# Squares and norms of an input check moved into the last product of a fused attention and feed-forward kernel

## The chip, the cores and the metric

The kernel runs on one core of a Trainium2 chip. A core has a matrix engine (TensorE, PE in the profile; its weight loads are PEld), a vector engine (VectorE, DVE), an activation engine (ScalarE, ACT), a general engine (GpSimd, POOL) and a sequencer for transfers (SyncE, SP). Each engine works through its own list of instructions in order and waits where an instruction needs something that another engine has not finished. Matrix products are summed in PSUM, a small memory in banks of 128 x 512 numbers of 32 bits; everything else on the chip is in SBUF. The metric is the device time of one execution in microseconds (us), and the median of several executions is compared.

## The reference

There are 8 batches of 576 tokens with 8 heads of 64. Attention sees a window of 32 positions to each side; 8 global positions see everything and are seen by everything. The result, 4608 tokens of 512 numbers, goes through a feed-forward layer with a periodic activation:

```python
scores = scale * np.matmul(q, k.transpose(0, 1, 3, 2))
mask = np.abs(pos[:, None] - pos[None, :]) <= window
mask = mask | is_global[:, None] | is_global[None, :]
scores = np.where(mask, scores, -1000000000.0)
attn = softmax(scores)                       # written out, with 1e-09 on the sum
x = np.matmul(attn, v)                       # then heads side by side: 4608 x 512

h = x @ w_in                                 # 512 x 2048
s = np.sin(alpha * h)
g = h + s * s / (alpha + 1e-09)
out = g @ w_out                              # 2048 x 512
```

## The kernel before, in words

The kernel walks over the batches in an order that is written out by hand. For batch b it does the attention (`attention(b, ...)`), then the first product with the activation (`gemm1(b)`), and the second product (`gemm2(b)`) is not done at once: it is a generator of single matmuls that stands in the list `waiting`. `fill(n)` takes n matmuls from that list and issues them, so that TensorE has something to do while the attention of the next batch waits for ACT and DVE. Attention b+1 thus runs with the second product of batch b in its gaps; `phase_a(b_att, b_moe)` sets up such a pair, and its inner function `beside(at)` issues small side jobs after head pair `at`.

**The first product** runs over 16 groups `nt` of 128 columns of w_in. A group takes 8 matmuls into one of three pairs of banks (`zn`, `zd`, and a third called `zr`), then a Sin on ACT out of PSUM, a square on ACT or DVE, and a multiply-add on DVE that writes H2, the input of the second product.

**The second product** takes blocks of 128 tokens: 16 matmuls of 512 columns into one of two banks, `zo[0]` or `zo[1]` in turn, then a copy `osb` on ACT (line 1048) and one or two output writes from SP (line 1055). The first matmul of a block waits until the copy two blocks earlier has emptied its bank. The generator issues a block's copy only when the matmul after it is asked for. After the last batch nothing is left to fill around: the rest of the second product of batch 6 (18 matmuls) and the five blocks of batch 7 (80 matmuls) run alone, followed by `gemm2_globals`, 16 matmuls for the global tokens, a copy, and an indirect write from POOL.

**The check.** Sin, exponentials and reciprocals are computed in a way that holds for moderate inputs only. So the kernel gathers evidence, and if any of it fails, it computes everything again in a slow general way (`general_path`). The pieces of that evidence are what the change moves:

- `square_w(c)`, four times: ACT squares a quarter of w_in, 2048 numbers per partition (line 888), and from the second on DVE adds the square to W2 (line 890). Before the change the first two stand in the first product of batch 1 (lines 995 and 996), the other two in attention 2 (lines 1132 and 1133).
- `column_norms`: 16 matmuls of one column sum W2 over partitions (line 895); five small DVE instructions make of it `limit`, the largest squared length that a token may have. It stands in attention 3 (lines 1119 and 1120).
- `square_x(b, part)`: DVE squares the tokens of a batch and halves them three times into SR, 288 columns (320 in the last batch, which carries the global tokens). This stays where it is.
- `token_norms(b, ...)`: one matmul sums SR over partitions, and DVE compares it with `limit` and counts (line 933). For batches 0 to 3 it stands in attentions 4 to 7 (lines 1121 and 1122), for batches 4 to 7 in the last product, after 32 of its matmuls.
- `judge`: a chain of small DVE instructions joins all evidence into one number, a matmul (line 952) sums it, and DVE writes `verdict`. It stands 16 matmuls further on. At the end every engine loads the verdict (line 1174) and branches (line 1175).

The end of the program before, for reference:

```python
    waiting.append(gemm2(B - 1))
    square_x(B - 1, 0)
    square_x(B - 1, 1)
    fill(32)
    for n, b in enumerate(sorted(SR)):
        token_norms(b, (zn, zd)[n % 2][:, 0, :])
    fill(16)
    judge(zn[:, 0, :])
    fill(2 * NT * NT)
    gemm2_globals()
```

Of the kernel before, what the change touches and what calls it, by code (L numbers as in the profile page):

```python
# [10 lines left out]
ALU = mybir.AluOpType  # L11
AF = mybir.ActivationFunctionType
DT = mybir.dt
# [3 lines left out]
P = 128  # L17
# [230 lines left out]
def kernel(  # L248
# [11 lines left out]
    nc = tc.nc  # L260
    B, H, S, D = q.shape
    DM, DFF = moe_w_in.shape
# [4 lines left out]
    CT = DM // P  # L267
    NT = DFF // P
    HALF = S // 2
# [11 lines left out]
    mctx = ExitStack()  # L281
    mctx.enter_context(tc.manual_schedule())
    dramp = mctx.enter_context(tc.tile_pool(name="dramp", bufs=2, space=bass.MemoryType.DRAM))
    main = mctx.enter_context(tc.tile_pool(name="main", bufs=1))
# [3 lines left out]
    xpool = mctx.enter_context(tc.tile_pool(name="xpool", bufs=1))  # L288
    spool = mctx.enter_context(tc.tile_pool(name="spool", bufs=3))
    osbp = mctx.enter_context(tc.tile_pool(name="osbp", bufs=3))  # L290
    srp = mctx.enter_context(tc.tile_pool(name="srp", bufs=4))

    VX = [main.tile([P, NHP, NT12, P], DT.bfloat16, name=f"VX{i}") for i in range(2)]
    KX = [main.tile([P, NHP, NT12, P], DT.bfloat16, name=f"KX{i}") for i in range(2)]
# [19 lines left out]
    limit = main.tile([P, 1], DT.float32, name="limit")  # L314
    EA = main.tile([P, B * NHP * 3], DT.float32, name="EA")
    RA = main.tile([P, B * NHP], DT.float32, name="RA")
    XC = main.tile([P, B], DT.float32, name="XC")
    XCG = main.tile([P, 1], DT.float32, name="XCG")


# [563 lines left out]

    def square_w(c):

        t = SQ[:, 0:DFF] if c else W2[:]
        nc.scalar.activation(out=t, in_=w_in[:, c, :], func=AF.Square)
        if c:
            nc.vector.tensor_tensor(out=W2[:], in0=W2[:], in1=t, op=ALU.add)  # L890
# [14 lines left out]
        )  # L905
        nc.vector.reciprocal(out=limit[:], in_=limit[:])

    SR = {}

    def square_x(b, part):  # L910

        W = HALF + (NE if b == B - 1 else 0)
        n = 2 * CT * W
        if part == 0:
            xf = xTs[b][:].rearrange("p c e s -> p (c e) s")[:, :, 0:W]
            nc.vector.tensor_tensor(
                out=SQ[:, 0:n].rearrange("p (g s) -> p g s", s=W), in0=xf, in1=xf, op=ALU.mult
            )
            return
        for m in (n // 2, n // 4):  # L920
            nc.vector.tensor_tensor(out=SQ[:, 0:m], in0=SQ[:, 0:m], in1=SQ[:, m : 2 * m], op=ALU.add)
        n //= 8
        SR[b] = srp.tile([P, n], DT.bfloat16, name="SR" if b < B - 1 else "SRl")
        nc.vector.tensor_tensor(out=SR[b][:], in0=SQ[:, 0:n], in1=SQ[:, n : 2 * n], op=ALU.add)

    def token_norms(b, pn):

        n = SR[b].shape[1]
        nc.tensor.matmul(out=pn[:, 0:n], lhsT=ones[:], rhs=SR.pop(b)[:], start=True, stop=True)
        for lo, hi, dst in ((0, HALF, XC[:, b : b + 1]), (HALF, n, XCG[:, 0:1])):  # L930
            if hi > lo:
                low = normp.tile([P, hi - lo], DT.bfloat16, name="low" if hi == HALF else "lowg")
                nc.vector.tensor_scalar(
                    out=low[:], in0=pn[:, lo:hi], scalar1=limit[:, 0:1], scalar2=0.0, op0=ALU.is_le,
                    op1=ALU.add, accum_out=dst,
                )

    def judge(pv):

        ok = [normp.tile([P, 1], DT.float32, name=f"ok{i}") for i in range(4)]  # L940
        for i, (src, lim, op) in enumerate(
            ((EA, LIM_SUM, ALU.is_le), (RA, LIM_REC, ALU.is_le), (XC, HALF - 0.5, ALU.is_ge),
             (XCG, NE - 0.5, ALU.is_ge))
        ):
            t = normp.tile(list(src.shape), DT.float32, name=f"cmp{i}")
            nc.vector.tensor_scalar(out=t[:], in0=src[:], scalar1=lim, scalar2=None, op0=op)
            nc.vector.tensor_reduce(out=ok[i][:], in_=t[:], axis=AX.X, op=ALU.min)
        nc.vector.tensor_tensor(out=ok[0][:], in0=ok[0][:], in1=ok[1][:], op=ALU.mult)
        nc.vector.tensor_tensor(out=ok[2][:], in0=ok[2][:], in1=ok[3][:], op=ALU.mult)
        okb = normp.tile([P, 1], DT.bfloat16, name="okb")  # L950
        nc.vector.tensor_tensor(out=okb[:], in0=ok[0][:], in1=ok[2][:], op=ALU.mult)
        nc.tensor.matmul(out=pv[:, 0:1], lhsT=ones[:], rhs=okb[:], start=True, stop=True)
        nc.vector.tensor_copy(out=verdict[:], in_=pv[:, 0:1])
# [6 lines left out]
    def gemm1(b):  # L960


        xT = xTs[b]
        r0 = (b % 2) * S
        more = b == B - 1
        W = HALF + (NE if more else 0)
        hr = tc.alloc_tile_pool(name="hr", bufs=1, space=PSUM)
        hs = {}

        order = "nrdonrdonrdnrdon" if b == 0 else "nrd" * 5 + "n"  # L970

        def chunks(nt, cs):
            if nt not in hs:
                if order[nt] == "o":
                    hs[nt] = [(slice(e, e + 1), zo[e][:, None, :]) for e in range(2)]
                else:
                    h = {"n": zn, "d": zd}.get(order[nt]) or hr.tile([P, 2, 512], DT.float32, name="zr")
                    hs[nt] = [(slice(0, 2), h[:])]
            h = [ap[:, i] for es, ap in hs[nt] for i in range(es.stop - es.start)]
            for c in cs:  # L980
                for e in range(2):
                    lhsT = w_in[:, c, nt * P : (nt + 1) * P]
                    nc.tensor.matmul(  # L983
                        out=h[e][:, 0:W], lhsT=lhsT, rhs=xT[:, c, e, 0:W],
                        start=(c == 0), stop=(c == CT - 1), skip_group_check=True,
                    )

        on_act = (ON_ACT_FIRST, ON_ACT_SECOND, ON_ACT)[min(b, 2)]
        for nt in range(NT):
            if b < 2 and 10 <= nt < 14:  # L990
                for which, t, y in PLACES[2 * (nt - 10) : 2 * (nt - 9)]:
                    place(b + 1, which, t, y, nc.vector.tensor_copy, slice(0, NHP if b else 2))
            if b == 1 and nt in (3, 4):
                square_x(0, nt - 3)
            if b == 1 and nt in (6, 8):
                square_w(nt // 2 - 3)
            if b == 0 and nt == 11:
                turn_kq()
            if b == 0 and nt == 11:

                load_w_out()
                cast_globals_v()
                place_globals(1)
                load_v(1, (2, 3))
                load_vg(1)
            if nt == 0:

                for n in range(2):
                    chunks(n, range(CT - 1))
            chunks(nt, range(CT - 1, CT) if nt < 2 else range(CT))  # L1010
            fill((GROUP_LATE if b == 1 else PER_GROUP)[nt])
            sb = spool.tile([P, 2, HALF + NE], DT.bfloat16, name="sb")
            s2 = spool.tile([P, 2, HALF + NE], DT.bfloat16, name="s2")
            for es, h in hs[nt]:
                nc.scalar.activation(  # L1015
                    out=sb[:, es, 0:W], in_=h[:, :, 0:W], func=AF.Sin, scale=alphaT[:, nt : nt + 1]
                )
            if nt in on_act:
                nc.scalar.activation(out=s2[:, :, 0:W], in_=sb[:, :, 0:W], func=AF.Square)  # L1019
            else:  # L1020
                nc.vector.tensor_tensor(out=s2[:, :, 0:W], in0=sb[:, :, 0:W], in1=sb[:, :, 0:W], op=ALU.mult)  # L1021
            for es, h in hs[nt]:
                nc.vector.scalar_tensor_tensor(  # L1023
                    out=H2[:, nt, r0 : r0 + S].rearrange("p (e c) -> p e c", e=2)[:, es],
                    in0=s2[:, es, 0:HALF], scalar=recipT[:, nt : nt + 1], in1=h[:, :, 0:HALF],
                    op0=ALU.mult, op1=ALU.add,
                )
            if more:
                nc.vector.scalar_tensor_tensor(
                    out=HG[:, nt, :].rearrange("p (x n) -> p x n", x=2),  # L1030
                    in0=s2[:, :, HALF:W], scalar=recipT[:, nt : nt + 1], in1=hs[nt][0][1][:, :, HALF:W],
                    op0=ALU.mult, op1=ALU.add,
                )
        hr.release()
# [43 lines left out]
    def fill(n):  # L1078
        while n and waiting:
            if next(waiting[0], None) is None:  # L1080
                waiting.pop(0)
            else:
                n -= 1
# [16 lines left out]
    def phase_a(b_att, b_moe):  # L1100
        def beside(at):

            if b_moe is None:
# [11 lines left out]
                    load_v(1, (0, 1))  # L1115
                    gather(v, gv)
                return
            if at == 0:
                if b_moe == 2:
                    column_norms(zn[:, 0, :])  # L1120
                if b_moe >= 3:
                    token_norms(b_moe - 3, zn[:, 1, :])
            if 0 <= at < 2 and b_moe:
                square_x(b_moe, at)
            if b_att == 1 and at == 0:
# [3 lines left out]
                place(b_att + 1, which, t, y, nc.vector.tensor_copy)  # L1129
            if b_moe == 0 and at == 2:  # L1130
                turn_qk(2)
            if b_moe == 1 and at in (2, 3):
                square_w(at)

        if b_moe is not None:
            waiting.append(gemm2(b_moe))
# [25 lines left out]
    waiting.append(gemm2(B - 1))  # L1162
    square_x(B - 1, 0)
    square_x(B - 1, 1)
    fill(32)
    for n, b in enumerate(sorted(SR)):
        token_norms(b, (zn, zd)[n % 2][:, 0, :])
    fill(16)
    judge(zn[:, 0, :])
    fill(2 * NT * NT)  # L1170
    gemm2_globals()
    mctx.close()

# [33 lines left out]
```

## Time and profile before

| What | Value |
|---|---|
| Median of 3 runs | 372.3 us (371.79 to 372.88) |
| Profiled execution, its own time | 373.89 us |
| Span of the profiled execution | 372.2 us |
| TensorE busy | 336.6 us, 90% of the span |
| ACT busy | 293.5 us, 79% |
| DVE busy | 282.8 us, 76% |
| Mean granted TensorE clock | 0.994 of full speed |
| Second product, line 1042 | 143.3 us, 530 matmuls recorded |
| Squares of w_in, line 888 | 4 instructions of 1.89 to 1.91 us, the first from 82.4 us, the last from 117.1 us |
| First sums of norms in the last product | from 346.29 us |

A span runs from the first to the last recorded instruction; the execution's own time contains it and some time around it. The busy time of an engine is an average over stages that are limited by different things, so it says little about a single move. The profile's timeline lists instructions in order of time: start, duration, engine, line, what is written from what, and in brackets how long the engine stood idle before and which engine released it. A matmul's duration includes its way through the array, so that matmuls overlap; their pace is read from start to start. Batches start their attention, by the first score matmul, at 98.69 (batch 2), 141.64, 181.19, 220.26, 259.44 and 298.61 us (batch 7).

### The profile page before, as it was taken

To read this page: it belongs to the slowest core of one execution; us is meant where nothing else is said; L and a number is where in the kernel's file an instruction comes from. 1 tells how busy PE (TensorE), PEld (TensorE's weight loads), DVE (VectorE), ACT (ScalarE), POOL (GpSimd) and SP (SyncE) were. 2 spreads that over 40 slices of the span, in tenths; PEclk is the share of its full clock that TensorE was granted. 3 is DMA by queue.
4 is the path that set the end of the run, shared out by engine and by line. 5 is a ranking of instruction groups with operands and counts; after the bars stand their busy time and mean duration, and the time that the engine had idled before them with its cause. 6 is when DMAs were issued, how large, how long until landed. Compare 5 with 4: busy or idle time off the path is not lost. (4 is left out here: it accounts for less than half of the span.)

```text
span 372.2 us, 8377 instructions
## 1 busy us (share of the span) xinstructions
PE 336.6 (90%) x2994; PEld 228.8 (61%) x3040; DVE 282.8 (76%) x624; ACT 293.5 (79%) x566; POOL 140.2 (38%) x246
## 2 busy tenths in 40 slices
PE   2578768998998899999999999999999999999993
PEld 1467556765565576667667766766676766655441
DVE  6777897588878888878888887888788876789500
ACT  7689896899889787888988797979888788876110
POOL 7893696679854700772066303730000000000001
PEclk9999998999999999999999999999999999999999
DMA  7999999999999445899089904646221001000221
GB/s 122 110 163 182 170 146 182 153 201 184 174 184 216 41 90 97 143 104 171 10 130 138 171 2 74 60 57 123 64 53 35 0 30 59 29 2 28 64 80 50
DMA packets 103579, 38.07 MB, mean 102 GB/s; under 512 B 94138, under 2 KB 98250, under 8 KB 103082
## 3 DMA queue, kind: packets, MB, share of 16 engines
q0 software_dynamic: 56640, 18.56, 43.2%
q1 hardware_dynamic: 46890, 18.89, 24.7%
q8 instruction: 26, 0.43, 0.5%
q14 instruction: 23, 0.19, 0.1%
HBM read 37.15 MB, written 17.83 MB: 148 GB/s over the span
## 5 line engine op out<-in xcount | busy, mean ns | idle before, releaser
L1042 PE MATMUL zo<-w_out,H 128*128 128x512 bf16 x530 | 143.3, 379 | 1.9
L983 PEld LDWEIGHTS <-w_in 128*128 128x128 bf16 x1024 | 98.6, 98 | 50.7 <-issue 13.2
L392 POOL DMA_DIRECT2D VX<-in_v_dram x128 | 82.9, 656 | 95.3 <-PE zd L782 71.3
L1042 PEld LDWEIGHTS <-H 128*128 128x128 bf16 x576 | 52.2, 97 | 37.9 <-issue 0.3
L748 ACT ACTIVATE E<-ring 128x480 bf16<-128x480 f32 x96 | 54.2, 567 | 22.6 <-PE ring L740 21.9
L751 DVE TENSOR_TENSOR E<-E,MASK 128x480 bf16<-128x480 bf16 x96 | 35.9, 405 | 16.2 <-ACT E L748 15.1
L1070 POOL DMA_INDIRECT out_dram<-osb,grow x1 | 1.0, 1001 | 121.6 <-SPq L1175 121.6
L1023 DVE SCALAR_TENSOR_TENSOR H<-s,recipT,zn 128x576 bf16<-128x576 bf16 x47 | 38.2, 814 | 9.0 <-ACT s L1019 5.6
L1019 ACT ACTIVATE s<-sb 128x576 bf16<-128x576 bf16 (+1 forms) x62 | 42.7, 689 | 2.0
L740 PE MATMUL ring<-QX,KX 128*128 128x120 bf16 x384 | 37.7, 224 | 7.0 <-ACT E L748 3.6
L1015 ACT ACTIVATE sb<-zn,alphaT 128x576 bf16<-128x576 f32 (+1 forms) x47 | 34.8, 740 | 11.3 <-PE zn L983 11.2
L740 PEld LDWEIGHTS <-KX 128*128 128x128 bf16 x384 | 28.8, 101 | 21.9 <-issue 10.7
L1023 DVE SCALAR_TENSOR_TENSOR H<-s,recipT,zd 128x576 bf16<-128x576 bf16 x39 | 31.7, 814 | 6.5 <-ACT s L1019 4.6
L1021 DVE TENSOR_TENSOR s<-sb 128x576 bf16<-128x576 bf16 (+1 forms) x66 | 30.5, 463 | 6.2 <-ACT sb L1015 5.9
L1048 ACT COPY osb<-zo 128x512 f32<-128x512 f32 x36 | 20.8, 576 | 18.3 <-PE zo L1042 18.2
L1023 DVE SCALAR_TENSOR_TENSOR H<-s,recipT,zr 128x576 bf16<-128x576 bf16 x39 | 31.7, 813 | 4.2 <-ACT s L1019 2.1
L1015 ACT ACTIVATE sb<-zd,alphaT 128x576 bf16<-128x576 f32 (+1 forms) x39 | 28.9, 740 | 6.9 <-PE zd L983 5.4
L1015 ACT ACTIVATE sb<-zr,alphaT 128x576 bf16<-128x576 f32 (+1 forms) x39 | 28.9, 740 | 4.7 <-PE zr L983 4.7
L782 PEld LDWEIGHTS <-VX 128*128 128x128 bf16 x448 | 26.2, 99 | 9.4 <-issue 3.3
L983 PE MATMUL zn<-xT,w_in 128*128 128x288 bf16 x184 | 26.9, 286 | 4.8 <-DVE H L1023 2.1
L983 PE MATMUL zn<-xlast,w_in 128*128 128x288 bf16 (+1 forms) x192 | 28.8, 289 | 0.7 <-DVE H L1023 0.2
L782 PE MATMUL zn<-E,VX 128*128 128x120 bf16 (+2 forms) x336 | 26.7, 211 | 1.0 <-DVE xlast L814 0.9
(161 smaller groups left out, 493.5 us busy)
## 6 DMA issues: line engine op xcount, KB each, us to landing
VX<-in_v_dram POOLq DMA_DIRECT2D x128, 36.0 KB, 5.6
kd<-in_k_dram POOLq DMA_DIRECT2D x7, 576.0 KB, 6.8
qd<-in_q_dram POOLq DMA_DIRECT2D x7, 576.0 KB, 9.0
w_in<-in_moe_w_in_dram POOLq DMA_DIRECT2D x4, 512.0 KB, 6.2
w_out<-in_moe_w_out_dram POOLq DMA_DIRECT2D x4, 512.0 KB, 8.8
out_dram<-osb SPq DMA_DIRECT2D x8, 256.0 KB
out_dram<-osb SPq DMA_DIRECT2D x8, 224.0 KB
out_dram<-osb SPq DMA_DIRECT2D x8, 192.0 KB
```

What stands on the lines that cost most here:

```text
L392: nc.gpsimd.dma_start(out=VX[b % 2][r : r + 24, hp, :, t * D : t * D + D], in_=v[b, 2 * hp + t].rearrange("(i a y) d -> y a i d", a=24, y= ...
L740: nc.tensor.matmul(out=ps[:, e * WCOL : (e + 1) * WCOL], lhsT=kx[:, hp, i, :], rhs=qx[:, hp, :, s0 : s0 + 60], start=True, stop=True, skip ...
L748: nc.scalar.activation(out=Eg, in_=ps[:, 0 : 4 * WCOL], func=AF.Exp, scale=scale, accum_out=EA[:, n : n + 1])
L751: nc.vector.tensor_tensor(out=Eg, in0=Eg, in1=MASK[:, 4 * g : 4 * g + 4, :].rearrange("p i c -> p (i c)"), op=ALU.mult,)
L782: nc.tensor.matmul(out=out_t[:, half, :, a - half * CUT : z - half * CUT], lhsT=OB[:] if key else VXb[:, hp, i, :], rhs=E[:, i, :, a - s0 ...
L983: nc.tensor.matmul(out=h[e][:, 0:W], lhsT=lhsT, rhs=xT[:, c, e, 0:W], start=(c == 0), stop=(c == CT - 1), skip_group_check=True,)
L1015: nc.scalar.activation(out=sb[:, es, 0:W], in_=h[:, :, 0:W], func=AF.Sin, scale=alphaT[:, nt : nt + 1])
L1019: nc.scalar.activation(out=s2[:, :, 0:W], in_=sb[:, :, 0:W], func=AF.Square)
L1021: nc.vector.tensor_tensor(out=s2[:, :, 0:W], in0=sb[:, :, 0:W], in1=sb[:, :, 0:W], op=ALU.mult)
L1023: nc.vector.scalar_tensor_tensor(out=H2[:, nt, r0 : r0 + S].rearrange("p (e c) -> p e c", e=2)[:, es], in0=s2[:, es, 0:HALF], scalar=recip ...
L1042: nc.tensor.matmul(out=ops[:], lhsT=H2[:, nt, blk * P : (blk + 1) * P], rhs=w_out[:, nt, :], start=(nt == 0), stop=(nt == NT - 1),)
L1048: nc.scalar.copy(out=osb[:], in_=ops[:])
```

## The change

All four squares of w_in, the column norms and the comparisons of all token norms move into the last product. Nothing of them is left in attentions or in first products; `square_x` stays, and the sums of all batches now stand side by side in one tile SR until the end.

- The four `square_w` are issued right after `square_x` of the last batch and before any matmul of the last product is filled. So on ACT they stand behind the last Sin and ahead of the copies of the last product. The second, third and fourth write their squares into KX[0], a key tile of the even batches, where before they used SQ.
- 44 matmuls of the second product are issued, then `column_norms` and the token norms of batches 0 and 1; then, with 10, 6 and 6 matmuls between them, those of batches 2 and 3, 4 and 5, and 6 and 7.
- The token norms of two batches go into the two halves of one PSUM tile, and one comparison counts both (three comparisons for batches 0 to 5, one each for 6 and 7, and one for the global tokens). Their written flags go into SQ instead of a tile of their own.
- `judge` has one more input, XP, with a comparison, a reduction and a product more. It now stands after all matmuls of the second product, ahead of the globals' product. On SP the load of the verdict comes to stand behind the last seven output writes; before, it stood ahead of them.

```diff
-    srp = mctx.enter_context(tc.tile_pool(name="srp", bufs=4))
...
-    XC = main.tile([P, B], DT.float32, name="XC")
+    SR = main.tile([P, B * HALF + NE], DT.bfloat16, name="SR")
+    XP = main.tile([P, B // 2 - 1], DT.float32, name="XP")
+    XC = main.tile([P, 2], DT.float32, name="XC")
...
     def square_w(c):
-        t = SQ[:, 0:DFF] if c else W2[:]
+        t = KX[0][:].rearrange("p h i c -> p (h i c)")[:, (c - 1) * DFF : c * DFF] if c else W2[:]
         nc.scalar.activation(out=t, in_=w_in[:, c, :], func=AF.Square)
         if c:
             nc.vector.tensor_tensor(out=W2[:], in0=W2[:], in1=t, op=ALU.add)
...
+    def token_norms(bs, pn):
+        for i, b in enumerate(bs):
+            n = HALF + (NE if b == B - 1 else 0)
+            nc.tensor.matmul(out=pn[:, i, 0:n], lhsT=ones[:], rhs=SR[:, sums_of(b)], start=True, stop=True)
+        b = bs[0]
+        cols = [(0, HALF, XP[:, b // 2 : b // 2 + 1] if len(bs) == 2 else XC[:, b % 2 : b % 2 + 1])]
+        if b == B - 1:
+            cols.append((HALF, HALF + NE, XCG[:, 0:1]))
+        for lo, hi, dst in cols:
+            m = len(bs) * (hi - lo)
+            nc.vector.tensor_scalar(
+                out=SQ[:, 0:m].rearrange("p (i c) -> p i c", i=len(bs)), in0=pn[:, 0 : len(bs), lo:hi],
+                scalar1=limit[:, 0:1], scalar2=0.0, op0=ALU.is_le,
+                op1=ALU.add, accum_out=dst,
+            )
...
-            if b == 1 and nt in (6, 8):
-                square_w(nt // 2 - 3)
...
-            if at == 0:
-                if b_moe == 2:
-                    column_norms(zn[:, 0, :])
-                if b_moe >= 3:
-                    token_norms(b_moe - 3, zn[:, 1, :])
...
-            if b_moe == 1 and at in (2, 3):
-                square_w(at)
...
     square_x(B - 1, 0)
     square_x(B - 1, 1)
-    fill(32)
-    for n, b in enumerate(sorted(SR)):
-        token_norms(b, (zn, zd)[n % 2][:, 0, :])
-    fill(16)
+    for c in range(CT):
+        square_w(c)
+    fill(44)
+    column_norms(zn[:, 0, :])
+    token_norms((0, 1), zd)
+    fill(10)
+    token_norms((2, 3), zn)
+    fill(6)
+    token_norms((4, 5), zd)
+    fill(6)
+    token_norms((6,), zn)
+    token_norms((7,), zd)
+    fill(2 * NT * NT)
     judge(zn[:, 0, :])
-    fill(2 * NT * NT)
     gemm2_globals()
```

## The prediction

> **What bounds the kernel now.** The page was read first, its 40 slices above all; then the timeline of each engine around the four squares of w_in's columns, then the timeline of the last 33 us, and last the stage windows for the TensorE clock.
>
> The page, part 2 (tenths of busy time per slice of 9.3 us):
> ```profile
> PE   2578768998998899999999999999999999999993
> ACT  7689896899889787888988797979888788876110
> PEclk9999998999999999999999999999999999999999
> ```
> TensorE is at nine tenths from slice 9 on, so work that only leaves ACT or DVE there is worth no more than the TensorE gaps that it causes. In the last three slices ACT is nearly empty and TensorE is full: the second product of the last batch is a plain run of matmuls at 0.216 us each (31 of them from 339.60 to 346.29).
>
> The timeline, ACT and TensorE, at the four squares (start, duration, engine, line, output<-input, idle before and its releaser):
> ```profile
> 85.44 1.90 ACT L888 ACTIVATE SQ<-w_in 128x2048 bf16<-128x2048 bf16 x1
> 86.37 1.14 PE L983 MATMUL zn<-xlast,w_in 128*128 128x288 bf16 x8 [0.20 <-DVE H L1023]
> 90.34 1.14 PE L983 MATMUL zd<-xlast,w_in 128*128 128x288 bf16 x8 [0.77 <-DVE H L1023]
> ...
> 111.77 1.89 ACT L888 ACTIVATE SQ<-w_in 128x2048 bf16<-128x2048 bf16 x1
> 113.57 0.55 ACT L748 ACTIVATE E<-ring 128x480 bf16<-128x480 f32 x1
> 114.26 0.37 PE L740 MATMUL ring<-QX,KX 128*128 128x120 bf16 x4 [0.48 <-ACT E L748]
> ...
> 117.14 1.91 ACT L888 ACTIVATE SQ<-w_in 128x2048 bf16<-128x2048 bf16 x1
> 118.95 0.73 ACT L808 ACTIVATE L<-zr,tiny 128x576 f32<-128x576 f32 x1
> 120.49 0.90 PE L983 MATMUL zr<-xT,w_in 128*128 128x288 bf16 x6 [1.02 <-DVE GS L792]
> ```
> Each square holds ACT for 1.80 us from start to next start, and TensorE stands still behind it a little later: these gaps are what the change can win.
>
> The timeline at the end, where the work goes:
> ```profile
> 339.60 6.85 PE L1042 MATMUL zo<-w_out,H 128*128 128x512 bf16 x31
> 339.88 0.78 ACT L1015 ACTIVATE sb<-zn,alphaT 128x640 bf16<-128x640 f32 x1
> 340.55 0.58 ACT L1048 COPY osb<-zo 128x512 f32<-128x512 f32 x1
> 343.47 0.58 ACT L1048 COPY osb<-zo 128x512 f32<-128x512 f32 x1 [2.34 <-PE zo L1042]
> 346.29 0.29 PE L929 MATMUL zn<-SR,ones 128*128 128x288 bf16 x1
> 347.77 2.54 PE L1042 MATMUL zo<-w_out,H 128*128 128x512 bf16 x11
> ```
> The copy at 340.55 empties the bank into which the block after next is summed. The second product has only two banks (zo), so no block starts before the copy of the block two before it.
>
> The stage windows of TensorE (PE busy, PEld, DVE, ACT, POOL, then PEclk, the granted clock):
> ```profile
> 52.00:56.00 4.00, 2.05 (x18) 1.27 (x17) 3.84 (x8) 3.94 (x8) 3.73 (x10) 1.00 1.20 195
> 56.00:57.00 1.00, 0.85 (x10) 0.59 (x9) 0.86 (x2) 1.00 (x5) 1.00 (x3) 0.89 1.33 211
> 57.00:60.00 3.00, 3.00 (x31) 2.34 (x29) 2.90 (x10) 1.55 (x6) 2.39 (x4) 0.50 1.34 210
> 60.00:61.00 1.00, 1.00 (x18) 0.88 (x16) 0.96 (x4) 0.57 (x2) 0.00 (x0) 0.90 1.58 170
> ```
> After a gap of 1.95 us (it ended at 54.90) the clock is half from 56.78 to 60.20 (0.22 us in one window, 3.00, 0.20 in the last).
>
> **The change part by part.** Its sum is made against the profiled execution: 373.89 us, span 372.2, that is 1.6 above the median of 372.3; the difference found is put on the median.
>
> *Squares out of the first product of batch 1* (two squares, one sum of 1.28 us on DVE). With three second-product matmuls between two groups the undisturbed step there is 1.63 us (91.75 to 93.38). The steps behind the squares are 1.98 (84.39 to 86.37) and 2.56 (87.78 to 90.34): 0.35 + 0.93 = 1.3 us won. From 91.75 to the end of this product TensorE never waits, so the gain stays.
>
> *Squares out of the attention of batch 2* (two squares, two sums of 1.23 us). Attention and first product run from the first score matmul to that of the next batch: 42.95 us for batch 2 (98.69 to 141.64), 39.55, 39.07, 39.18 and 39.17 for batches 3 to 6. Less 0.41 for its column norms, batch 3 takes 39.14; batch 2 is 3.81 above it. Not all is the squares': batch 2 places four query blocks on DVE after its last normalisation (2.22 us), batch 3 two, so 1.1 stays. Won: 2.7 us. Bounds: 1.5 (0.48 and 1.02, the two waits shown) to 3.8.
>
> *Column norms out of attention 3, token norms of batches 0 to 3 out of attentions 4 to 7.* The 16 small matmuls take TensorE from 145.50 to 145.91, 0.41 us; each token-norm matmul 0.13 (185.05 to 185.18): 0.41 + 4 x 0.13 = 0.93 won. Their DVE work (five small instructions of 0.83 together, four comparisons of 0.51 + 0.08) lies beside dense matmuls: attentions 4 to 7 with a comparison last 18.83 to 19.09, attention 3 without one 18.71, so the matmul is nearly all that it costs.
>
> *Four squares in front of the evictions.* This is the dear step. On ACT the squares stand right behind the last Sin (339.88) and ahead of every copy of the second product. Their sources are long loaded and KX0 has no reader left after batch 6, so they start at 340.55 and the first copy starts 4 x 1.80 later, at 347.75, and ends at 348.33. TensorE has 18 matmuls to do without it (two of one block, 16 of the next), until 339.60 + 18 x 0.216 = 343.49; then it waits until about 348.43: **4.94 us** of stall. Behind that wait stand the whole of the last five blocks, the norms and the globals' product. Bounds: 4.9 to 5.4 (squares at their full 1.91).
>
> *The clock after it.* No gap of this length is in the trace. From below nothing: a gap of 1.92 us at 41.07 to 42.99 left the clock at 1.00. From above 3.4, two stretches of half clock. I take the nearest row in kind, 56.78 to 60.20: 3.42 us at half speed, 1.7 us lost. The Trainium skill ("TensorE: Matmul & The Clock Gate", Part 1) puts the drop to 1.2 GHz after at least one idle window of about 3.4 us, and the return after a busy one. By that rule the 1.95 us gap could not have dropped the clock, and the trace shows that it did; taken strictly, it would leave the sum without the 1.7 wherever no whole window fits into the stall.
>
> *Norms in the last product.* Column norms 0.41 and eight token-norm matmuls of 0.13, 1.04. In their place go the four norms of before, which cost 346.29 to 347.77, 1.48, mostly waits for the comparisons. These waits do not come back: ten and six matmuls (2.16 and 1.30 us) lie between the pairs, over comparisons of 576 columns, between one and two of 0.51. The three sums on DVE end near 349.3, before TensorE asks for W2 at about 355: hidden by 26 matmuls, and up to 3.7 us if these were gone.
>
> *Verdict.* Its DVE chain (1.8 us, three instructions of about 0.16 more) runs beside the last 32 matmuls (6.9 us). On SP the load of the verdict is now behind seven output writes instead of ahead of them; it took 0.47 us, and SP's last issue ends at 363.2 while the globals' 16 matmuls and their copy run to 366.43. Nothing.
>
> Sum: -1.3 - 2.7 - 0.93 + 4.94 + 1.7 + 0.41 + 1.04 - 1.48 = **+1.7 us**. Median 374.0, profiled execution 375.6.
>
> **The rivals.**
> A. *The clock stays full.* Sum without 1.7: 0.0, so 372.3. For it: the gap at 41.07. Against: the half clock after 54.90, behind a gap of two fifths of this one.
> B. *Half clock twice as long,* because the stretch in which the matmuls resume is itself half empty: 1.7 more, 375.7. For it: the drop came 1.9 us after matmuls had resumed at 54.90, so the idle part of a stretch counts against it. Against: a dense run follows here, and in the trace one stretch was enough.
> C. *Batch 2 gives nothing back.* DVE's four query copies stay, and TensorE waits 1.43 for DVE at 125.47; if that chain does not start earlier, 2.7 is lost: 376.7. Against: the chain begins with the reduction of zr, which waits for the logarithm behind the square at 117.14.
> D. *Faster: ACT is the true bound of the early stages* (20.17 of 22 us busy from 76 to 98, 21.65 of 24 from 98 to 122) and returns every square in full: 4 x 1.80 = 7.2 instead of 4.0, so 374.0 - 3.2 = 370.8. It decides once these stages give over 6.8. Against: all of batch 2's excess and the 1.3 are 5.1.
>
> **How the numbers follow.** Forecast 0.45 (own range 372.9 to 375.2), A 0.15, B 0.17, C 0.13, D 0.10. A measurement of this kernel tells 0.3%, 1.1 us, from no change. Slower: B, C and four fifths of the forecast, 0.66; same: the rest of it and most of A, 0.21; faster: D and a little of A, 0.13. The range takes in A and B, C's end nearly and half of D: 371.3 to 376.8.
>
> **What would show it.** ACT: four squares of 1.9 in a row after the last Sin, the copy after them. TensorE: a gap near 4.9 us in the last 32 us, released by that copy, and PEclk below 1 in the slice behind it. Batch 2 from scores to scores near 40.2. Column norms with no wait before them, the verdict's matmul neither. The prediction is wrong if the gap is short, if the clock holds, or if batches 1 and 2 give over 5 us or under 2.

## The result and the profile after

The changed kernel took 374.35 us (median of 6 executions, 374.06 to 375.54) against 372.05 for the kernel before (6 executions, 371.79 to 372.88): a ratio of 1.0064, 95% interval 1.0047 to 1.0081. That is 2.3 us more, 1.75 to 3.0. On another chip it was 374.88 against 373.0, ratio 1.0065 (1.0044 to 1.0086). Every ratio below is against the kernel before on the same chip, whose median was 372.05 to 373.07; an expected time that starts from 372 is read with that in mind.

The profile of the changed kernel, part 2 of its page (span 372.6 us, slices of 9.3 us):

```profile
PE   1678769999998999999999999999999999994993
ACT  7799897888878788878888888888888988788110
PEclk9999998999999999999999999999999999998998
```

What is new is the 4 in TensorE's row, three slices from the end, and the 8 below it: in the last product TensorE now stands still, and behind that its clock is lower. Both were 9 before. (The 8 in the last slice lies behind the last matmul, which ends at 366.30.)

The timeline of the changed kernel in the last product, ACT and TensorE (start, duration, engine, line, output<-input, idle before and its releaser; the lines of the Sin, the squares, the copies and the second product are now 1020, 889, 1053 and 1047):

```profile
333.42 4.05 PE L1047 MATMUL zo<-w_out,H 128*128 128x512 bf16 x18
333.91 0.78 ACT L1020 ACTIVATE sb<-zn,alphaT 128x640 bf16<-128x640 f32 x1
334.58 1.90 ACT L889 ACTIVATE W<-w_in 128x2048 bf16<-128x2048 bf16 x1
336.38 5.50 ACT L889 ACTIVATE KX<-w_in 128x2048 bf16<-128x2048 bf16 x3
341.79 1.05 ACT L1053 COPY osb<-zo 128x512 f32<-128x512 f32 x2
342.40 7.27 PE L1047 MATMUL zo<-w_out,H 128*128 128x512 bf16 x26 [4.94 <-ACT osb L1053]
349.51 0.54 PE L896 MATMUL zn<-ones,W 128*128 128x1 bf16 x16
355.65 7.07 PE L1047 MATMUL zo<-w_out,H 128*128 128x512 bf16 x32
362.56 0.17 PE L959 MATMUL zn<-okb,ones 128*128 128x1 bf16 x1
```

After the last Sin come the four squares, then two copies back to back. TensorE does the 18 matmuls that need no copy and then waits 4.94 us for the first one. From the first of the 18 to the first behind the wait it is 8.98 us, 5.09 more than 18 x 0.216: a bracket counts only from the modelled end of the matmul before. The 26 matmuls behind the wait take 7.11 us to the column norms where 26 x 0.216 would be 5.6. Column norms and the verdict's matmul start with no wait of their own.

The stage windows of the changed kernel around the gap (PE busy, PEld, DVE, ACT, POOL, then the granted clock):

```profile
330.00:342.00 12.00, 7.47 (x42) 3.80 (x41) 11.07 (x18) 11.40 (x11) 0.00 (x0) 1.00 0.00 0
342.00:345.50 3.50, 3.10 (x8) 1.13 (x8) 1.47 (x3) 0.84 (x2) 0.00 (x0) 0.51 0.47 147
345.50:366.00 20.50, 20.50 (x115) 9.90 (x112) 6.36 (x31) 2.93 (x5) 0.00 (x0) 1.00 0.22 67
```

Only 8 matmuls were done in 3.10 busy microseconds: the clock is half for 3.4 us and full before and after.

The places that were freed, in the timeline of TensorE in the changed kernel:

```profile
85.12 1.14 PE L990 MATMUL zn<-xlast,w_in 128*128 128x288 bf16 x8
88.16 1.14 PE L990 MATMUL zd<-xlast,w_in 128*128 128x288 bf16 x8
...
115.28 0.90 PE L990 MATMUL zn<-xT,w_in 128*128 128x288 bf16 x6
116.01 0.90 PE L990 MATMUL zr<-xT,w_in 128*128 128x288 bf16 x6
...
120.59 1.14 PE L990 MATMUL zn<-xT,w_in 128*128 128x288 bf16 x8 [1.13 <-DVE H L1028]
```

The waits of 0.20, 0.77 and 1.02 us that stood at the same groups are gone; zr follows zn after 0.73 us. The last line is the wait for DVE's four query copies; it stays.

Batch 1's first product now lasts 24.89 us (26.13 before). From first score matmul to first score matmul, batch 2 takes 40.25 (42.95), batches 3 to 6 together 155.96 (156.97); batch 7, up to the last product, 40.65 (40.99). From there to the end of the span it is 39.18 (32.60). So -1.24 - 2.70 - 1.01 - 0.34 + 6.58 = +1.3 us between these two profiles, while their spans differ by 0.4 only, because the first product of batch 1 happened to start at 71.67 in the one and at 72.56 in the other. Of such single profiles more are needed; they come with the experiments. One flaw of the first pair has to be known: its profile of the kernel before lacks a record. It shows 31 matmuls from 339.60 to the first norm at 346.29, where the program issues 32; in another profile of the same kernel (c_before_again) all 32 are there, in 6.90 us up to that norm:

```profile
338.48 7.07 PE L1042 MATMUL zo<-w_out,H 128*128 128x512 bf16 x32
```

So the last product of the first profile began near 339.39, 0.2 us earlier than read, and the last two terms above are rather -0.13 and +6.37.

### The profile page after: what moved, and what is told of

Same layout as the page of the kernel before. It is cut to its first block, busy times and chain, and to the rows that moved or that the text cites. A ratio compares the mean times of both kernels' runs of the same rounds, so it can differ in the third digit from the quotient of the medians.

```text
span 372.6 us, 8428 instructions
## 1 busy us (share of the span) xinstructions
PE 338.7 (91%) x3040; PEld 228.7 (61%) x3040; DVE 282.8 (76%) x621; ACT 293.9 (79%) x566; POOL 138.3 (37%) x246
## 5 line engine op out<-in xcount | busy, mean ns | idle before, releaser
L1047 PE MATMUL zo<-w_out,H 128*128 128x512 bf16 x576 | 155.4, 382 | 4.9 <-ACT osb L1053 4.9
```

Source lines behind the costliest of these rows:

```text
L1047: nc.tensor.matmul(out=ops[:], lhsT=H2[:, nt, blk * P : (blk + 1) * P], rhs=w_out[:, nt, :], start=(nt == 0), stop=(nt == NT - 1),)
```

## The experiments

The theory: the early stages give back the gaps of TensorE and no more (4 us for the squares, 1 for the norms), and the last product pays 4.9 us for copies that wait behind the squares and some 1.5 to 1.7 for the clock that falls in that gap. Rivals: the norms, not the squares, are what costs there; the matmuls are slow for another reason than the gap; ACT gives back every square in full.

**The squares in the last product, but between its copies.**

```diff
-    for c in range(CT):
-        square_w(c)
-    fill(44)
+    fill(4)
+    square_w(0)
+    square_w(1)
+    fill(16)
+    square_w(2)
+    square_w(3)
+    fill(32)
     column_norms(zn[:, 0, :])
     token_norms((0, 1), zd)
-    fill(10)
+    fill(8)
```

> The changed kernel, with the four squares still in the last product but two behind its first copy and two behind its second, column norms after 52 of its matmuls and the verdict as in the changed kernel. Theory (the copies wait behind the squares): no gap of TensorE over 0.5 us in the last product, no copy late, the clock stays full there, so 4.9 + 1.5 come off the changed kernel: 367.9 us, 4 under the kernel before. Rival (the last product is slow because of the work that came into it, wherever it stands): the gap only moves, to the column norms or to a later block, and the time stays within 1.5 us of the changed kernel, 373 to 376.

Measured: 368.72 us against 373.07, ratio 0.9884 (0.9851 to 0.9917), 4.3 us under the kernel before. The timeline of ACT and TensorE in this kernel:

```profile
334.54 11.39 PE L1047 MATMUL zo<-w_out,H 128*128 128x512 bf16 x52
345.77 0.54 PE L896 MATMUL zn<-ones,W 128*128 128x1 bf16 x16
...
335.71 0.57 ACT L1053 COPY osb<-zo 128x512 f32<-128x512 f32 x1
336.18 1.92 ACT L889 ACTIVATE W<-w_in 128x2048 bf16<-128x2048 bf16 x1
337.99 1.91 ACT L889 ACTIVATE KX<-w_in 128x2048 bf16<-128x2048 bf16 x1
339.79 0.58 ACT L1053 COPY osb<-zo 128x512 f32<-128x512 f32 x1
340.26 3.73 ACT L889 ACTIVATE KX<-w_in 128x2048 bf16<-128x2048 bf16 x2
343.87 0.59 ACT L1053 COPY osb<-zo 128x512 f32<-128x512 f32 x1
```

52 matmuls run in one piece at 0.216 us each, with all four squares beside them. The work is the same and stands in the same product; its place against the copies differs, and the norms come 6 to 8 matmuls later. The rival falls: between the copies the added work makes TensorE wait nowhere, and the order on ACT makes the whole difference. This kernel is faster than both, as expected (367.9 from a start of 372).

**TensorE kept busy in the gap.**

```diff
-    fill(44)
+    fill(18)
+    warm(zd[:, 0, :], 22)
+    fill(26)
```

> The changed kernel, with 22 matmuls on constants put into the gap (4.75 us at 0.216), so that TensorE is busy while it waits for the first copy. The output is the same. Theory (the idle gap halves the clock): granted clock 1.00 in the last product, the first real matmul at the same distance behind the last Sin, and 1.5 us less than the changed kernel, 372.8 us. Rival (matmuls are slow there for another reason, or the stall alone is the cost): still 0.43 us from start to start for the first matmuls behind the gap, time unchanged at 374.3, or longer by what the added matmuls push back.

Measured: 373.23 us against 373.07, ratio 1.0004 (0.9990 to 1.0018); the changed kernel stood at 1.0064, so 2.2 us are gone where 1.5 were expected; further profiles of the changed kernel, below, put the slow matmuls at 1.9 us on average. Timeline of TensorE in this kernel:

```profile
337.75 4.91 PE L545 MATMUL zd<-ones 128*128 128x512 bf16 x22
342.85 5.77 PE L1047 MATMUL zo<-w_out,H 128*128 128x512 bf16 x26 [0.19 <-ACT osb L1053]
348.46 0.54 PE L896 MATMUL zn<-ones,W 128*128 128x1 bf16 x16
```

The real work resumes 9.0 us after the first of the 18 matmuls (333.86 to 342.85), as in the changed kernel (333.42 to 342.40): the wait for the copy is untouched. But the 26 matmuls now take 5.61 us, and the granted clock is 1.00 throughout the last product. That holds beyond the profiled execution: over the whole span the mean granted clock is 0.992 to 0.997 in the 12 executions of this kernel and 0.978 to 0.991 in the 18 of the changed one. So the stall and the clock are two costs, and the second is gone when TensorE isn't idle in the gap.

**The norms late, the squares where they were.** (Squares two to four are written to SQ again, as before.)

```diff
...
             if b == 1 and nt in (3, 4):
                 square_x(0, nt - 3)
+            if b == 1 and nt in (6, 8):
+                square_w(nt // 2 - 3)
...
+            if b_moe == 1 and at in (2, 3):
+                square_w(at)
...
-    for c in range(CT):
-        square_w(c)
     fill(44)
```

> The changed kernel with the four squares left where they stood before, in batch 1's first product and attention 2; column norms and all token norms in the last product. Theory: attentions 3 to 7 give 0.9 to 1.4 us, the last product gains a little (its waits for comparisons are gone), no gap, so 370.9 us, 1 to 1.4 under the kernel before. Rival (the norms in the last product are what costs): 373 us or more.

Measured: 371.36 us against 373.07, ratio 0.9946 (0.9928 to 0.9965), 1.7 us less, 1.3 to 2.7, where 1 to 1.4 were expected. Batch 2 takes 42.86, as before; batches 3 to 6 take 156.24, batch 7 up to the last product 40.65, the last product 32.48. Against the averages of the kernel before, in the table below, that is 0.8, 0.2 and 0.2 us less, 1.2 together. So the norms are a gain by themselves, by these stages of the size expected; the rest of the 1.7 is not placed by this profile.

**The kernel before without squares.** The squares and their sums are left out, and the column norms sum a part of w_in as it is, so a term of the input check is missing.

```diff
-            if b == 1 and nt in (6, 8):
-                square_w(nt // 2 - 3)
...
-            if b_moe == 1 and at in (2, 3):
-                square_w(at)
...
-                out=pw[:, nt : nt + 1], lhsT=W2[:, nt * P : (nt + 1) * P], rhs=ones[:, 0:1],
+                out=pw[:, nt : nt + 1], lhsT=w_in[:, 0, nt * P : (nt + 1) * P], rhs=ones[:, 0:1],
```

> The kernel before without the four squares and their three sums; the column norms then sum w_in's first quarter as it is, so one term of the input check is not computed. It measures what the early stages give back by themselves. Theory (only the gaps of TensorE come back): 1.3 in batch 1's first product and 2.7 in batch 2, so 368.0 us, and batch 2 from its first score matmul to that of batch 3 takes 40.2. Rival (ACT is the bound of these stages and every square comes back in full): 7.2 us, 364.8.

Measured: 369.93 us against 373.07, ratio 0.9915 (0.9896 to 0.9933): 3.1 us less, 2.5 to 3.9. The theory had said 4.0. Batch 1's first product takes 24.91, batch 2 40.56: 1.2 and 2.3 less than on average before, where 1.3 and 2.7 were expected. So 7.2 us of ACT work, and the three sums on DVE with it, taken out of stages in which ACT is over 90% busy (20.17 of 22 us and 21.65 of 24) return about half of it. A full return is excluded.

**Two squares late, and three.** (With two late, the second square is written to SQ, as before.)

```diff
...
+            if b == 1 and nt in (6, 8):
+                square_w(nt // 2 - 3)
...
-    for c in range(CT):
+    for c in range(2, CT):
         square_w(c)
```

> The changed kernel with two of the four squares left in batch 1's first product, as before, and two in the last product. Theory (each late square delays the first copy by 1.80 us): gap of TensorE in the last product 4.94 - 3.60 = 1.3 us. The clock most likely holds over so short a gap, then the time is 4.9 - 1.3 + 1.5 below the changed kernel less the 1.3 not won in batch 1: 1.5 us under the kernel before; if the clock falls all the same, as it did once behind a gap of 1.95 us, equal to it. Rival (the gap is not made by the squares one by one, but by the wait for W2 or the banks): gap near 4.9 or none.

```diff
+            if b == 1 and nt == 6:
+                square_w(0)
...
-    for c in range(CT):
+    for c in range(1, CT):
         square_w(c)
```

> The changed kernel with the first square left in batch 1's first product, three in the last product. Gap by 1.80 a square: 3.1 us. It asks what length halves the clock. If half a stretch of 3.4 us without work is enough: half clock for one stretch behind the gap, 0.5 to 1.0 us over the kernel before. If a whole stretch without work is needed: clock full, 0.7 under the kernel before.

Measured: 370.41 us with two (ratio 0.9930, 0.9905 to 0.9955) and 373.18 with three (1.0006, 0.9986 to 1.0026), against 373.0. Two late squares save 2.6 us where 1.5 were expected. With three, the clock answers the question (half for one stretch), while the time, 0.2 us over the kernel before, lies a little under the 0.5 to 1.0 that went with that answer. The line behind the gap and the stage windows, two squares late first:

```profile
340.27 5.77 PE L1049 MATMUL zo<-w_out,H 128*128 128x512 bf16 x26 [1.35 <-ACT osb L1055]
...
340.20:344.00 3.80, 3.73 (x18) 1.72 (x18) 3.33 (x6) 0.59 (x3) 0.00 (x0) 1.00 0.44 138
```

Three squares late:

```profile
341.53 7.46 PE L1049 MATMUL zo<-w_out,H 128*128 128x512 bf16 x26 [3.15 <-ACT osb L1055]
...
341.50:345.00 3.50, 3.47 (x9) 1.31 (x9) 2.79 (x4) 0.47 (x1) 0.00 (x0) 0.52 0.48 150
```

The gap is 1.35, 3.15 and 4.94 us with two, three and four squares: 1.80 and 1.79 for one more. From two to three the time rises by 2.8 us, more than the square itself: 1.8 for the gap, 1.7 for the clock (26 matmuls in 7.30 us instead of 5.61), less 0.84 won in batch 1 (26.10 to 25.26).

**Both kernels profiled again.**

> The changed kernel unchanged, on the same chip as the two above, for comparison: 2.3 us over the kernel before, gap 4.9 us, half clock for one stretch behind it.

Measured: 374.88 against 373.0, as above; gap 4.94 us, 26 matmuls in 7.29 us.

> The kernel before unchanged, profiled once more. Batch 2 takes 42.95 us again from scores to scores, batches 3 to 6 39.1 to 39.6. The start, up to the first matmul of batch 0's first product at 32.77, may move by some tenths of a microsecond; how far the span moves with it tells how much two single profiles can be compared.

> The kernel before, a further profile, for the time of the first matmul of batch 1's first product (72.56 and 71.76 us in the two so far). If the start merely scatters, 71 to 73 here too; if the changed kernel starts later by itself, below 71.5.

> The kernel before, one more profile for the same time: 71 to 73 us if the start merely scatters, below 71.5 if the changed kernel starts later by itself.

> The changed kernel, a further profile, for the same time (71.67 and 72.38 us in the two so far). Scatter alone: 71 to 73 and no further apart from the kernel before than its own profiles are from one another.

Single executions of the kernel before took 373.55, 372.58 and 375.72 us, one more of the changed kernel 376.54. The first product of batch 1 starts at 72.56, 71.76, 71.81 and 74.62 in the kernel before and at 71.67, 72.38 and 72.26 in the changed one: scatter, larger within one kernel than between the two, and the fourth lies outside what was expected. What follows it hardly scatters, so the parts can be averaged over four and three profiles:

| us | before | changed | difference |
|---|---|---|---|
| Batch 1, first product | 26.13 | 24.98 | -1.15 |
| Batch 2, scores to scores | 42.81 | 40.25 | -2.56 |
| Batches 3 to 6 | 157.06 | 155.97 | -1.09 |
| Batch 7 to the last product | 40.83 | 40.65 | -0.18 |
| Last product to the end | 32.69 | 39.61 | +6.92 |

The sum is +1.9 us, and the medians say +1.9 and +2.3. (The missing record shifts the last two rows by 0.05.) No stage outside the table is needed for the difference. The third profile of the changed kernel has the longest end, 40.4 us, for this reason (timeline and stage windows):

```profile
343.44 8.38 PE L1047 MATMUL zo<-w_out,H 128*128 128x512 bf16 x26 [4.95 <-ACT osb L1053]
...
342.00:345.50 3.50, 2.06 (x5) 0.71 (x5) 2.50 (x3) 1.88 (x3) 0.00 (x0) 0.50 0.27 83
345.50:349.00 3.50, 3.50 (x10) 1.31 (x9) 0.00 (x0) 0.00 (x0) 0.00 (x0) 0.53 0.21 67
```

Here the clock was half for 6.8 us, two stretches of 3.4, and the 26 matmuls took 8.22 us.

## Why the prediction was right

It forecast 374.0 us, 1.7 over the kernel before, and slower at 0.66; the kernel came out at 374.35, 2.3 over, 1.9 on the second chip. The mechanism was the forecast one: the gaps of the early stages came back, and the stall and the clock behind it cost more. By its own steps:

- *Squares out of batch 1* (1.3): 1.24 in the first pair, 1.15 on average, 1.2 where only the squares are left out. Right; the steps of 1.98 and 2.56 us are now 1.63.
- *Squares out of batch 2* (2.7): 2.70, on average 2.56, and 2.3 where only the squares are left out. Right, if a little large, and the part set aside as not the squares' is there: TensorE still waits 1.13 us for DVE at the group after zd.
- *Norms out of the attentions* (0.93): 1.14 in the first pair (1.01 and 0.13), 1.2 to 1.3 on average. A little small.
- *Squares ahead of the evictions* (4.94 us): the brackets say 4.94, 4.94 and 4.95, and the gap is made by the squares one by one. The mechanism was right; that the figure fits to the hundredth is luck. The sum ran from 339.60 in starts of matmuls. From 339.39, where the last product must have begun, it gives 5.15, and what was lost from start to start is 5.09.
- *The clock* (1.7): 1.50, 1.68 and 2.61 us in three profiles, 1.9 on average. The mechanism was right, and the size is not one number. The case of rival B, half clock for twice as long, occurs in some executions; in the one seen it cost 0.9 more than 1.7, since 1.5 us of the first stretch fell into the stall. The misses of the other steps (0.15 and 0.14 too much expected of the squares, 0.3 too little of the norms, 0.15 too little for the stall) nearly cancel, and that is luck. What the forecast was short by on the second chip, 0.2, is then the size of the clock's 0.2; the 0.6 on the first chip no profile places.
- *Norms in the last product* (0.41 and 1.04, in place of 1.48): 0.41 and 0.97, with no wait for a comparison, as forecast.
- *Verdict* (nothing): its last DVE instruction ends at 359.14 and its matmul starts at 362.56, right behind the second product. From the globals' first matmul to the end of the span it is 9.5 to 10.6 us in the four profiles of the kernel before and 9.9 to 10.0 in the three of the changed one.

Rival A fell: the clock dropped in each of the three profiles. It was weighed down because of the half clock behind a gap of 1.95 us in the trace of before, and that weighing came out: the gap of 3.15 us with three late squares halved the clock too, while 1.35 did not. The Trainium skill's "after" condition in "TensorE: Matmul & The Clock Gate", Part 1, is one idle window of about 3.4 us. The traces differ, since 3.15 us is shorter than that. But the row that the prediction leaned on was no sure guide either. In the third profile of the changed kernel the same gap of 1.95 us, before batch 1's scores, left the clock at 1.00 (timeline and stage window):

```profile
55.38 0.37 PE L741 MATMUL ring<-QX,KX 128*128 128x120 bf16 x4 [1.95 <-POOL QX L376]
...
52.00:60.00 8.00, 5.49 (x62) 3.71 (x61) 7.62 (x19) 6.84 (x16) 7.55 (x16) 1.00 1.25 196
```

Rival C fell, since DVE's chain began earlier with the logarithm, as argued: ACT starts the logarithm of zr 17.80 us after the batch's first score matmul, 20.26 before the change. Rival D fell by its own experiment.

Two readings of the page were loose, with nothing in the sum resting on them. TensorE is not at nine tenths everywhere from slice 9 on: slices 10, 13 and 14 show 8, and there lie the gaps behind the squares and the wait for DVE (of these only slice 13 still shows 8 in the changed kernel). And of the last three slices, in which it is called full, the last shows 3.

## What to carry to other kernels

Work that is moved to a stage with an idle engine has to be placed against what that engine owes to the others, instruction by instruction: the same four squares made the kernel 6.6 us slower ahead of two copies than between them (2.3 over and 4.3 under the kernel before). Take the work out of its old place alone, as a kernel of its own, before counting on it: what returns is the gaps of the bounding engine (3 to 4 us of 7.2 here), not the busy time removed. And a stall of TensorE is priced with the slow matmuls behind it: here a third to a half of the stall again for 3.15 and 4.94 us, nothing for 1.35.

## What was not expected of the hardware

- How long the clock stays half differs from execution to execution of one kernel, in whole stretches: 3.4 us (342.05 to 345.47), 3.4 (343.28 to 346.69) and 6.8 (341.92 to 348.76), read from windows of 0.02 us. In the first two, matmuls resumed at most 0.35 us after the clock fell, in the third 1.52 us after it; a stretch that is almost half idle seems to be followed by another at half clock, but there is one such case only.
- The times at which the clock changes lie on one grid. In the first profile of the changed kernel they are 55.33, 58.74, 342.05, 345.47 and, after the work, 369.35 us: 0, 1, 84, 85 and 92 steps of 3.413 us. In the third they are 341.92, 348.76 and 372.64: 0, 2 and 9 steps. So the stretches run on by themselves and do not begin with a gap; where a gap falls on the grid may thus decide what it does. That fits the free-running window of which the Trainium skill speaks in Part 1 of the page named above, "TensorE: Matmul & The Clock Gate". How much of a stretch has to be idle is not shown: of the five gaps of 1.95 or 1.96 us ahead of batch 1's scores in the profiles of these two kernels, four were followed by half clock and one was not.
- The start of the kernel, up to batch 1's first product, scatters by nearly 3 us between profiles of the same kernel (71.76 to 74.62). Two single spans can therefore hide a change of this size, as the first pair did (372.2 and 372.6), while the stages after it agree to some tenths. In the latest of the four the clock was half in two stretches before that point (44.43 to 47.86 and 58.09 to 61.50), in the others in one or none; but one with a stretch (71.81) starts as early as the one without (71.76), so what makes the scatter stays open.
